# The gV and gK stores of the last head in two parts each: 120 rows and 8 rows

## The chip, the core and the metric

The kernel runs on one core of a Trainium2 chip. The metric is the device time of one execution, in microseconds (us). Engines are named as the profile names them: PE (TensorE matmul) and PEld (its weight loads), DVE (VectorE), ACT (ScalarE), POOL (GpSimd) and SP (SyncE, which here only issues transfers). Sixteen DMA engines move the data between HBM and the core's SBUF (the on-chip memory of 128 partitions). A DMA instruction of any of the issuing engines is cut up over them, and it adds 16 to a semaphore when all of it has landed.

## The reference

The program is the gradient of one decoder block for a single new token: LayerNorm, attention over a cache of 4096 positions, a residual, LayerNorm, a two-layer ReLU network, a residual. There are 2 batch entries, 32 heads of width 128, a model width of 640 and a hidden width of 1728, all in bf16.

```python
scores = jnp.einsum("bhqd,bhkd->bhqk", q, k) * (Dh ** -0.5)
p = _softmax(scores, axis=-1)
o = jnp.einsum("bhqk,bhkd->bhqd", p, v)
...
h  = x + A(_layernorm(x), k_cache, v_cache, wq, wo)
h2 = h + B(_layernorm(h), w1, w2)
...
_out, _vjp = jax.vjp(_f, A_x, A_k_cache, A_v_cache, A_wq, A_wo, B_w1, B_w2)
_grads = _vjp(grad_out)
```

The outputs are `h2` and seven gradients. The two large ones are the gradients of the K cache (`out_2`) and of the V cache (`out_3`), each of 2 x 32 heads x 4096 x 128 bf16. With one query per head they are outer products: for one head, gV is `p` (4096 numbers) times a row of 128 numbers, and gK is the gradient of the scores times the query row.

## The kernel before, in words

A head's 4096 x 128 matrix is 1 MB. It is held as one tile of 128 partitions by 32 x 128 numbers, so that a partition holds 32 consecutive positions, 8192 bytes that are contiguous in HBM (`natural`, line 451).

Pass 1 (`p1_iter`) goes over the 64 heads (`NP1`), reads K and V, forms the scores, the softmax numerators and some sums. A middle part (`middle_gen`) does the network and its gradients. Pass 2 (`p2_iter`, with its delayed second half `p2_tail`) goes over the 64 heads again in the order `turns`; most V tiles are loaded once more ("W"), some were kept. For each head `j` pass 2

- transposes V on PE and multiplies it by the output gradient (`pair_transpose`, `pair_matvec`),
- builds gV on DVE in two halves (`outer_half`, line 832). In the last three heads DVE leaves the last four of the 32 position blocks to ACT (line 899). GpSimd then issues the store of gV to `out_3` (line 900),
- in `p2_tail`, one head later, forms the score gradient `gsp` on DVE (line 843), builds gK in two halves (line 832), and GpSimd issues the store of gK to `out_2` (line 851).

In this way 128 stores of 1 MB go out from GpSimd's queue, gV and gK in turn. The tiles are taken from a set of homes (`take`, `give`) and a home is written again when the store that read it has landed. The framework that records the program gives GpSimd's stores eight semaphores in turn, and has a store wait until the store that used its semaphore before, eight stores earlier, has landed. The last two stores are those of head 63: gV of line 900 at `j == NP1 - 1`, and gK of line 851, which is issued when `p2_tail(NP1 - 1)` runs after the last `p2_iter`.

Beside the two passes, background generators hand out small pieces of work: `fin_gen` makes the weight gradients, stored from ACT's queue, and `gx_gen` makes the gradient of the input and ends with two stores of 5 rows from SP's queue (`store_row`, line 653). When all is issued, SP waits for all outstanding transfers and the engines meet at a barrier (the instructions under line 1288, the kernel's call).

Of the kernel before, what the change touches and what calls it, by code (L numbers as in the profile page):

```python
# [15 lines left out]
def kernel(  # L16
# [20 lines left out]
    nc = tc.nc  # L37
# [36 lines left out]
    def pst(shape, dtype, role, name):  # L74

        k = banks[role].pop(0)
        banks[role].append(k)
        return ps.tile(shape, dtype, tag=f"bank{k}", bufs=1, name=name)
# [11 lines left out]
    def take(tag, shape, name):  # L90
        assert free[tag] > 0, (tag, name)
        free[tag] -= 1
        k = homes[tag].pop(0)
        t = pools[k].tile(shape, BF16, tag=f"big{k}", bufs=1, name=name)
        home_of[id(t)] = (tag, k, t)
        return t
# [9 lines left out]
    def give(t, to=None):  # L106
        tag, k, _ = home_of.pop(id(t))
        to = to or goes_to(tag)
        owned[tag] -= 1
        owned[to] += 1  # L110
        free[to] += 1
        homes[to].append(k)
        given_at[k] = step[0]
# [288 lines left out]
    NP1 = len(pairs)  # L402
# [24 lines left out]
    def pair_transpose(nat, g, dve=False, busy=0):  # L427


        t_ps = pst([128, GT // 2, 128], FP32, "tps", "t_ps")  # L430
        warm(t_ps[:].rearrange("p j k -> p (j k)"), nat, g, busy)
        natf = nat[:].bitcast(FP32)
        for j in range(GT // 2):
            cc = (g * GT) // 2 + j
            nc.tensor.transpose(t_ps[:, j, :], natf[:, 2 * cc:2 * cc + 2, :].rearrange("p c k -> p (c k)"), ident_f[:])  # L435
        t_sb = mats.tile([128, GT // 2, 128], FP32, tag="XT", bufs=4, name="t_sb")
        if dve:
            nc.vector.tensor_copy(out=t_sb[:], in_=t_ps[:])  # L438
        else:
            nc.scalar.copy(out=t_sb[:], in_=t_ps[:])  # L440
        return t_sb

    def pair_matvec(dst, t_sb, g, vecs):
        v = t_sb[:].bitcast(BF16).rearrange("p j (k two) -> p j k two", two=2)
        for j in range(GT // 2):
            sc = g * GT + 2 * j
            for par in range(2):
                nc.tensor.matmul(dst[:, sc:sc + 2], lhsT=v[:, j, :, par], rhs=vecs[:, par, :],  # L448
                                 start=(par == 0), stop=(par == 1))

    def natural(cache, b, h):
        return cache[b, h].rearrange("(p sc) d -> p sc d", sc=NSC)
# [377 lines left out]
    def outer_half(dst, row, colp, k, n=HALF):  # L830
        sl = slice(k * HALF, k * HALF + n)
        nc.vector.tensor_tensor(  # L832
            out=pairs_view(dst[:, sl, :]),
            in0=row.rearrange("p (a two) -> p a two", two=2)[:, None, :, :].to_broadcast([128, n, 64, 2]),
            in1=colp[:, sl, None, :].to_broadcast([128, n, 64, 2]), op=ALU.mult)

    def p2_tail(j):

        p = S2[j]
        bp, hp = turns[j]  # L840
        pair_matvec(p["dp"], p.pop("T3"), 3, gom[:, bp, hp, :, :])
        gsp = small.tile([128, NSC, 2], BF16, tag="gsp", bufs=2, name="gsp")
        nc.vector.scalar_tensor_tensor(
            out=gsp[:], in0=p["dp"][:, :, None].to_broadcast([128, NSC, 2]), scalar=negdot[:, hp, bp:bp + 1],
            in1=P_bf[:, p_slot[(bp, hp)], :, None].to_broadcast([128, NSC, 2]), op0=ALU.add, op1=ALU.mult)
        yield
        gK = take("g", [128, NSC, 128], "gK")
        outer_half(gK, p["rb"][:, 128:256], gsp, 0)
        yield
        outer_half(gK, p["rb"][:, 128:256], gsp, 1)  # L850
        nc.gpsimd.dma_start(out=natural(out_2, bp, hp), in_=gK[:])  # L851
        give(gK)
        del S2[j]
        yield
# [3 lines left out]
    def p2_iter(j, nsb):  # L858

        tail = p2_tail(j - 1) if j - 1 in S2 and "T3" in S2[j - 1] else iter(())  # L860
        c = S2[j]
        next(tail, None)
        b, h = turns[j]
        go = gom[:, b, h, :, :]
        bank = pst([128, 512], FP32, "sps", "dp_ps")
        for k, col in enumerate((goc, qsc)):
            nc.tensor.matmul(bank[:, 128 + k * 128:256 + k * 128],  # L867
                             lhsT=col[:, h, b:b + 1].to_broadcast([128, 128]), rhs=ident_bf[:],
                             start=True, stop=True)
        c["dp"] = bank[:, 0:NSC]  # L870
        rb = mats.tile([128, 256], BF16, tag="rb", bufs=3, name="rb")
        nc.scalar.activation(out=rb[:], in_=bank[:, 128:384], func=ACT.Copy, scale=rt[:, b, h:h + 1])  # L872
        pp = small.tile([128, NSC, 2], BF16, tag="pp", bufs=2, name="pp")
        nc.gpsimd.tensor_copy(out=pp[:], in_=P_bf[:, p_slot[(b, h)], :, None].to_broadcast([128, NSC, 2]))
        if nsb:
            pf = small.tile([128, NSB], FP32, tag="pf", bufs=2, name="pf")
            nc.gpsimd.tensor_copy(out=pf[:, 0:nsb], in_=P_bf[:, p_slot[(b, h)], NSC - nsb:NSC])
        c.update(rb=rb, pp=pp)
        c["T0"] = pair_transpose(c["W"], 0)
        next(tail, None)  # L880
        yield
        for _ in tail:
            yield
        c["T1"] = pair_transpose(c["W"], 1)
        pair_matvec(c["dp"], c.pop("T0"), 0, go)
        yield
        c["T2"] = pair_transpose(c["W"], 2)
        pair_matvec(c["dp"], c.pop("T1"), 1, go)
        yield
        c["T3"] = pair_transpose(c["W"], 3)  # L890
        give(c["W"], "g" if j < H and j != 1 and owned["g"] < 3 else None)
        pair_matvec(c["dp"], c.pop("T2"), 2, go)
        gV = take("g", [128, NSC, 128], "gV")
        outer_half(gV, c["rb"][:, 0:128], c["pp"], 0)
        yield
        outer_half(gV, c["rb"][:, 0:128], c["pp"], 1, HALF - nsb)
        if nsb:
            for k in range(nsb):
                nc.scalar.activation(out=gV[:, NSC - nsb + k, :], in_=rb[:, 0:128], func=ACT.Copy, scale=pf[:, k:k + 1])
        nc.gpsimd.dma_start(out=natural(out_3, b, h), in_=gV[:])  # L900
        give(gV)
        yield

# [266 lines left out]
    for n, (i, j) in enumerate(plan):  # L1170
# [22 lines left out]
        if j is not None:  # L1193
            if j < NP1:
                bg_until(("go", *turns[j]))
            nsb = 0 if i is not None else NSB if j < H and fin is None else NSB // 2 if j >= NP1 - 3 else 0
            g2 = p2_iter(j, nsb) if j < NP1 else p2_tail(NP1 - 1)
        elif open_tail:
            g2 = p2_tail(open_tail[0])
# [93 lines left out]
```

## Time and profile before

| what | us |
|---|---|
| three timed runs: median (lowest to highest) | 898.54 (893.46 to 898.84) |
| the profiled execution, its own time | 896.3 |
| its span, first to last instruction | 894.4 |
| DVE busy | 688.1 (77% of the span) |
| PE busy | 740.6 (83%) |
| ACT busy | 469.5 (52%) |
| POOL busy | 198.6 (22%) |

The page counts 361.84 MB moved in 56304 packets, 405 GB/s on average. In its row of 40 slices the DMA engines show 9 tenths or more in every slice but two, one of 7 in the second quarter and the last one of 6. Reading starts at the DMA side for this reason. The page's times are of one execution. A view by windows gives, for a stretch of time, the busy time of each engine, the granted PE clock and the mean busy share of the 16 DMA engines (a share of 0.0625 is one engine of sixteen).

### The profile page before, as it was taken

How to read it: one execution, taken by the hardware profiler on the slowest of the kernel's cores; microseconds unless marked ns; L12 is line 12 of the kernel's file. 1: busy time of each engine (PE TensorE's matmuls, PEld its weight loads, DVE VectorE, ACT ScalarE, POOL GpSimd, SP SyncE). 2: the span in 40 equal slices, each digit the busy share in tenths (PEclk: the TensorE clock that was granted, in tenths of full speed). 3: DMA queues.
4: the chain of work that ended last, by engine and by line, in shares of the span. 5: the costliest groups of instructions: out<-in, count | busy, mean ns of one | idle time of the engine just before them, and what ended most of it. 6: DMA issues, size and time to landing. Idle time of an engine off the chain costs nothing.

```text
span 894.4 us, 24636 instructions
## 1 busy us (share of the span) xinstructions
PE 740.6 (83%) x10145; PEld 622.7 (70%) x10145; DVE 688.1 (77%) x1283; ACT 469.5 (52%) x1184; POOL 198.6 (22%) x342
## 2 busy tenths in 40 slices
PE   4999899999998998897867887875698988858881
PEld 4887788888887887777757776764566765635570
DVE  2666778976888897796678897877988468898992
ACT  1344334443555665464545776553476666537751
POOL 1344434442210000000011231111222111111141
PEclk9999989999999999898995555555657566555655
DMA  9999999999979999999999999999999999999996
GB/s 377 420 412 403 409 407 418 411 414 410 356 299 366 422 422 424 422 422 423 414 382 390 416 416 418 414 412 422 398 394 423 426 421 424 423 426 424 423 423 256
DMA packets 56304, 361.84 MB, mean 405 GB/s; under 512 B 5696, under 2 KB 11904, under 8 KB 15488
## 3 DMA queue, kind: packets, MB, share of 16 engines
q1 hardware_dynamic: 34536, 211.13, 58.1%
q0 software_dynamic: 18432, 134.23, 36.1%
q10 hardware_dynamic: 3224, 14.92, 4.0%
q8 instruction: 80, 1.31, 0.6%
q14 instruction: 32, 0.26, 0.1%
HBM read 211.11 MB, written 149.13 MB: 403 GB/s over the span
## 4 chain that ended last, share of the span: by engine, by line
DMA 37%; PE 31%; DVE 19%; issue 6%; ACT 3%; POOL 1%; SPq 0%; POOLq 0%; DVEq 0%; ACTq 0%
DMA out_dram<-gK 16%; PE t_ps L435 13%; DMA Vt<-in_A_v_cache_dram 12%; PE m_ps L469 7%; DMA out_dram<-gV 5%; DVE gV L832 5%; DVE gK L832 4%; DVE rows L658 4%; PE s_ps L448 3%; DVE pk L476 3%; DMA wo_t<-in_A_wo_dram 2%; PE u_ps L498 2%; DMA Kt<-in_A_k_cache_dram 2%; PE dp_ps L448 2%; ACT t_sb L440 1%
## 5 line engine op out<-in xcount | busy, mean ns | idle before, releaser
L440 ACT COPY t_sb<-t_ps 128x512 f32<-128x512 f32 x479 | 272.6, 587 | 181.3 <-PE t_ps L435 177.0
L448 PEld LDWEIGHTS <-t_sb 128*128 128x128 bf16 x4096 | 169.7, 103 | 75.1 <-ACT t_sb L440 33.3
L435 PE MATMUL t_ps<-ident_f,Wt 128*128 128x128 f32 x832 | 200.0, 392 | 0.4 <-ACT t_sb L440 0.4
L476 DVE TENSOR_TENSOR pk<-Kt,ep 128x2048 bf16<-128x2048 bf16 x128 | 156.3, 1222 | 44.7 <-ACT ep L523 26.0
L469 PE MATMUL m_ps<-pk,Vt 128*128 128x129 bf16 x2048 | 175.8, 224 | 15.0 <-DMA Vt<-in_A_v_cache_dram 14.4
L832 DVE TENSOR_TENSOR gK<-rb,gsp 128x2048 bf16<-128x2048 bf16 x128 | 153.4, 1224 | 18.5 <-DMA out_dram<-gV 16.9
L832 DVE TENSOR_TENSOR gV<-rb,pp 128x2048 bf16<-128x2048 bf16 (+2 forms) x128 | 147.1, 1172 | 23.6 <-DMA out_dram<-gK 23.1
L435 PEld LDWEIGHTS t_ps<-ident_f,Wt 128*128 128x128 f32 x832 | 140.2, 204 | 32.1 <-issue 26.5
L435 PE MATMUL t_ps<-ident_f,Kt 128*128 128x128 f32 x1024 | 153.4, 285 | 3.7 <-DMA Kt<-in_A_k_cache_dram 3.5
L469 PEld LDWEIGHTS <-Vt 128*128 128x128 bf16 x2048 | 130.9, 100 | 18.1 <-DMA Vt<-in_A_v_cache_dram 16.1
L435 PEld LDWEIGHTS t_ps<-ident_f,Kt 128*128 128x128 f32 x1024 | 116.3, 148 | 5.1 <-issue 2.6
L486 POOL COPY pk<-ep 128x16 bf16<-128x16 bf16 x80 | 83.6, 1047 | 152.3 <-ACT ep L523 107.0
L448 PE MATMUL dp_ps<-gom,t_sb 128*128 128x2 bf16 x2048 | 96.0, 168 | 14.5 <-ACT t_sb L440 14.1
L900 POOL DMA_DIRECT2D out_dram<-gV x64 | 34.3, 536 | 317.7 <-DVE gV L832 115.6
L448 PE MATMUL s_ps<-gom,t_sb 128*128 128x2 bf16 x2048 | 80.2, 164 | 1.2 <-DVE t_sb L438 1.2
L851 POOL DMA_DIRECT2D out_dram<-gK x64 | 34.1, 533 | 200.3 <-DVE gK L832 149.6
L582 ACT CAST MT<-m_ps 128x128 bf16<-128x128 f32 x64 | 17.0, 266 | 116.3 <-PE m_ps L469 116.3
L965 ACT CAST ot<-o_ps 128x512 bf16<-128x512 f32 (+3 forms) x152 | 66.8, 494 | 8.9 <-DMA out_dram<-ot 7.3
L872 ACT ACTIVATE rb<-dp_ps,rt 128x256 bf16<-128x256 f32 x64 | 30.3, 474 | 45.5 <-PE dp_ps L867 43.2
L658 DVE CUSTOM_DVE_ANT_0 rows<-wo_t,rows 128x640 bf16<-128x640 bf16 x64 | 52.3, 818 | 0.2
L658 DVE CUSTOM_DVE_ANT_0 rows<-wqs,gqr 128x1024 bf16<-128x1024 bf16 x40 | 48.8, 1220 | 0.2
L658 DVE CUSTOM_DVE_ANT_0 rows<-w_t,rows 128x640 bf16<-128x640 bf16 (+2 forms) x58 | 45.9, 792 | 2.8 <-ACT rows L636 2.1
(194 smaller groups left out, 715.7 us busy)
## 6 DMA issues: line engine op xcount, KB each, us to landing
Kt<-in_A_k_cache_dram SPq DMA_DIRECT2D x64, 1024.0 KB, 16.5
Vt<-in_A_v_cache_dram SPq DMA_DIRECT2D x64, 1024.0 KB, 16.6
out_dram<-gV POOLq DMA_DIRECT2D x64, 1024.0 KB, 14.1
out_dram<-gK POOLq DMA_DIRECT2D x64, 1024.0 KB, 14.3
Wt<-in_A_v_cache_dram SPq DMA_DIRECT2D x52, 1024.0 KB, 11.4
out_dram<-ot ACTq DMA_DIRECT2D x6, 960.0 KB, 12.7
wq_t<-in_A_wq_dram SPq DMA_DIRECT2D x5, 1024.0 KB, 11.0
wqs<-in_A_wq_dram SPq DMA_DIRECT2D x5, 1024.0 KB, 22.2
```

Source lines behind the costliest of these rows:

```text
L435: nc.tensor.transpose(t_ps[:, j, :], natf[:, 2 * cc:2 * cc + 2, :].rearrange("p c k -> p (c k)"), ident_f[:])
L440: nc.scalar.copy(out=t_sb[:], in_=t_ps[:])
L448: nc.tensor.matmul(dst[:, sc:sc + 2], lhsT=v[:, j, :, par], rhs=vecs[:, par, :], start=(par == 0), stop=(par == 1))
L469: nc.tensor.matmul(r["m"][:, 0:129], lhsT=r["V"][:, sc, :], rhs=r["pk"][sc // HALF][:, sc % HALF, 0:129], start=(sc == 0), stop=(sc == NSC ...
L476: nc.vector.tensor_tensor(out=p["pk"][k][:, :, 0:128].rearrange("p s (a two) -> p s a two", two=2), in0=p["K"][:, sl, :].rearrange("p s (a ...
L486: nc.gpsimd.tensor_copy(out=col, in_=e)
L658: nc.vector.tensor_tensor_reduce(out=junk[0:kc, 0:width], in0=in0, in1=in1, scale=1.0, scalar=0.0, op0=ALU.mult, op1=ALU.add, accum_out=acc)
L832: nc.vector.tensor_tensor(out=pairs_view(dst[:, sl, :]), in0=row.rearrange("p (a two) -> p a two", two=2)[:, None, :, :].to_broadcast([128 ...
L851: nc.gpsimd.dma_start(out=natural(out_2, bp, hp), in_=gK[:])
L872: nc.scalar.activation(out=rb[:], in_=bank[:, 128:384], func=ACT.Copy, scale=rt[:, b, h:h + 1])
L900: nc.gpsimd.dma_start(out=natural(out_3, b, h), in_=gV[:])
L965: nc.scalar.copy(out=ot[0:P, k, n0:n0 + nn], in_=o_ps[0:P, 0:nn])
```

## The change

A helper `store` is added in front of `p2_tail`. For all heads but the last it issues the same single store as before. For the last head it issues two: rows (partitions) 0 to 119, then rows 120 to 127, both from GpSimd's queue.

```diff
+    def store(dst, t, last):
+
+        if not last:
+            nc.gpsimd.dma_start(out=dst, in_=t[:])
+            return
+        for rows in (slice(0, 120), slice(120, 128)):
+            nc.gpsimd.dma_start(out=dst[rows], in_=t[rows])
+
     def p2_tail(j):
...
-        nc.gpsimd.dma_start(out=natural(out_2, bp, hp), in_=gK[:])
+        store(natural(out_2, bp, hp), gK, j == NP1 - 1)
...
-        nc.gpsimd.dma_start(out=natural(out_3, b, h), in_=gV[:])
+        store(natural(out_3, b, h), gV, j == NP1 - 1)
```

In the built program the instructions of PE, DVE and ACT are the same in number, order and waits. GpSimd's last two stores of 128 rows become four, of 120, 8, 120 and 8 rows. They take the next four of the eight semaphores, so that the third one waits for the landing of the gV store of head 60 and the fourth for the gK store of head 60. SP's last wait asks for these two semaphores at the higher count.

## The prediction, written before the changed kernel was run

> **What bounds the kernel at its end.** I began with the critical chain, the work that ended last, because the change touches only the last two of 128 stores. Its end (start us, length us, what):
>
> ```profile
> 873.32 0.91 DVE gV L832
> 874.23 1.80 issue
> 876.03 0.02 POOLq L851
> 876.05 0.53 POOL out_dram L900
> 876.58 1.72 issue
> 878.30 0.56 POOLq L1288
> ```
>
> No engine works after 878.9 but the span ends at 894.4. The last 15.5 us are transfers. The view of waits from 860 to 895 us, for SP's queue, names them (total us, times, longest):
>
> ```profile
> SPq L1288 <- DMA out_dram<-gV: 19.2, 1, 19.2
> SPq L1288 <- DMA out_dram<-gK: 2.4, 1, 2.4
> ```
>
> SP's closing wait ends first on the gV stores, then 2.4 us later on the last gK. The issues of gK (line 851) in this stretch give the times:
>
> ```profile
> L851 POOL DMA_DIRECT2D out_dram<-gK x4: 533/533/533, 864.1 to 878.3; - x4
> ...
> DMA to landing us min/median/max: 14.0/14.1/14.4
> ```
>
> The last gK is issued at 878.3 and lands 14.4 us later, at 892.7; closing takes 1.7 us more, and 1.9 us lie outside the span (896.3 in all). Next, how many of the 16 DMA engines still work. The windows view (stretch, its length, busy time of PE, PEld, DVE, ACT, POOL, granted clock, DMA share, GB/s):
>
> ```profile
> 880.00:882.00 2.00, 0.00 (x0) 0.00 (x0) 0.00 (x0) 0.00 (x0) 0.00 (x0) 0.50 1.00 418
> 882.00:884.00 2.00, 0.00 (x0) 0.00 (x0) 0.00 (x0) 0.00 (x0) 0.00 (x0) 0.50 0.96 406
> 884.00:886.00 2.00, 0.00 (x0) 0.00 (x0) 0.00 (x0) 0.00 (x0) 0.00 (x0) 0.50 0.54 229
> 886.00:888.00 2.00, 0.00 (x0) 0.00 (x0) 0.00 (x0) 0.00 (x0) 0.00 (x0) 0.50 0.17 70
> 888.00:890.00 2.00, 0.00 (x0) 0.00 (x0) 0.00 (x0) 0.00 (x0) 0.00 (x0) 0.50 0.08 33
> 890.00:892.00 2.00, 0.00 (x0) 0.00 (x0) 0.00 (x0) 0.00 (x0) 0.00 (x0) 0.50 0.07 29
> ```
>
> All 16 engines work until 883, half of them are done by 886, and for the last 4 us the share is 0.07, one engine of sixteen. One engine is behind the rest, and its rows of the last gV and gK alone set the end. Followed packet by packet (each starts when its engine's one before ends), the last engine ends at 892.30, the next ones at 888.35, 887.79 and 886.27, the first at 883.29. So the tail is an imbalance of queues, and the question is how many rows the change leaves on that one engine.
>
> **The price of a row.** The page's account of GpSimd's queue:
>
> ```profile
> q0 software_dynamic: 18432, 134.23, 36.1%
> ```
>
> 18432 packets by 128 stores are 144 a store: 128 rows of 8192 bytes and 16 end marks, so 8 rows and a mark for each engine. The 2.4 us between the last two landings are 8 rows on the last engine: 0.31 us a row by its packets (0.309 each, started every 0.306).
>
> **The change, part by part.**
>
> Two more issues on POOL, 0.53 us each. The 8 rows of gV go out at 876.58 to 877.11, inside the 1.72 us in which POOL waits for DVE's second half of gK; the 120 rows of gK still go at 878.33. The 8 rows of gK follow at 878.9 to 879.4, and nothing stands behind them on POOL. Their cover is the backlog: the emptiest DMA engine has rows until 883.3, the last one until it reaches the last gV at 887.4. If these issues took 2 us each, the last would end near 882, still in time. Price 0; without the backlog it would be 0.5.
>
> Two added waits. The third store waits for the gV store of the timeline's first row here, the fourth for the gK store of the second:
>
> ```profile
> 861.45 0.53 POOL L900 DMA_DIRECT2D out_dram<-gV  x1 [2.83 <-DVE gsp L843]
> 861.97 0.73 POOL L874 COPY pp<-P_bf 128x64 bf16<-128x64 bf16 x1
> 862.64 1.18 POOL L877 CAST pf<-P_bf 128x4 f32<-128x4 bf16 x1
> 864.08 0.53 POOL L851 DMA_DIRECT2D out_dram<-gK  x1 [0.25 <-DVE gxo L1059]
> ```
>
> With their 14.1 us to landing these end at 875.6 and at 878.1, before 878.3 and 878.9. The second has only 0.8 us to spare, but only SP's closing wait is behind it, and 4 us of backlog cover a delay. Price 0.
>
> The rows themselves. No row of the trace shows a 120-row or an 8-row store, so I bound it. The count of rows stays 256. If the 120 rows go to 15 engines they are 8 each, as before, and one engine gets none; 8 rows on 8 engines are one more each. The last engine then has 0 to 18 rows of the two stores, where it had 16. The upper end is 2 x 0.306 = +0.6 us. At the lower end its queue ends 16 rows or 4.9 us earlier, 887.4, and the next engine, 888.35 with up to two rows more, 889.0, is last: 892.3 - 889.0 = -3.3 us.
>
> Which end? The nearest rows are the only partial stores near the end, two of 5 rows from SP. In the stretch from 860 to 895 us the account of their queue is
>
> ```profile
> q1 hardware_dynamic: 20, 0.00, 0.0%
> ```
>
> that is 10 packets for each: 5 rows and 5 marks on five engines. Both times they are the same five by the packets, and the last engine is one of them. If GpSimd's partial stores fill engines in the same fixed order, an engine that a 5-row store takes is also among the 15 of a 120-row store and the 8 of an 8-row store. The one left out lies at the other end. So I take the upper end, +0.6 us.
>
> The Trainium skill (DMA: Bandwidth & Descriptors, section Why a DMA increments its semaphore by 16 and not by 1) says that a transfer from SP takes the lowest-numbered engines, as many as divide its rows, and that some GpSimd copies on trn2 put a sixteenth of the partitions, rounded up, on each engine in order, so that 100 partitions leave engine 15 without data. By these two rules 120 rows leave out engine 15, the last engine here is one of 0 to 4, and the sum is the same +0.6.
>
> The Trainium skill's Rules for kernel authors (same title) speak against the change: a transfer split by partitions gains nothing, because the parts share the same engines. With the backlog above, the split would cost the added rows and nothing else.
>
> **Sum.** 896.3 + 0 + 0 + 0.6 = 896.9 us. The profiled execution lies 2.2 below the median of the three runs and 2.8 above the lowest, about the middle of all four, so I leave the sum as it is.
>
> **Rivals.**
>
> *The last engine is spared in both stores.* It is the engine that a 120-row store leaves out. For it: 120 = 15 x 8, so some engine is left out, and an engine that is late in every store of the last heads may stand at a special place, such as the end of the row. Against it: it carries the five-row stores. 896.3 - 3.3 = 893.0 us. The Trainium skill (DMA: Bandwidth & Descriptors, Latency and other measured facts) calls engines 7 and 15 usually the slower ones; if the last engine were 15, this rival would hold.
>
> *It is spared in one store only.* The engine left out moves on from store to store and is the last one in one of the two. It has then 8 rows and up to two more instead of 16: 6 x 0.306 = 1.8 us less, 894.5 us. For it: the gV store of 15 engines and the 8-row store behind it need not begin at the same engine. Against it: by chance alone two stores hit one engine of sixteen 1 time in 8.
>
> *The rows pile up on few engines (slower).* If the number of engines must be a power of two, 120 rows go to 8 engines with 15 each, and the last engine, if it is among them, has 30 + 2 rows instead of 16: 16 x 0.306 = +4.9, 901.2 us. On 4 engines it has 60 + 2: 46 x 0.306 = +14.1, 910.4 us. On one engine 240 rows take 73 us. It counts as slower by over 1% (9.0 us) from 30 rows more on the last engine (30 x 0.306 = 9.2), that is from 5 engines or fewer for 120 rows. For it: every GpSimd store of this trace went to 16 engines, so none shows another number. Against it: SP's 5-row stores used five engines, which is no power of two.
>
> That the change doesn't do what it says is excluded by the order of the built program: four stores in place of two, nothing else moved.
>
> More than 6.7 us can't be gained: the shares from 880 on (1.00 + 0.96 + 0.54 + 0.17 + 0.08 + 0.07) x 2 us sum to 5.6 us of all engines, so even a perfect spread ends at 885.6 instead of 892.3.
>
> **How the numbers follow.** Forecast, the last engine keeps its rows (896.9): 0.54. Spared in both (893.0): 0.30. Spared in one (894.5): 0.10. Piling up: 0.06, of which 0.04 over 1%. The three runs lie from 2.8 below to 2.5 above the profiled one, which gives 890.2 to 899.4 over the first three cases; I take 891.5 to 900.0 for 8 in 10, since few of the spared cases fall on the lowest runs and the mildest piling up reaches 901. 1% (9 us) is about what a measurement of this kernel tells from no change. A gain of that size is beyond the bound above: faster 0.02, for scatter alone. Slower 0.05, the 0.04 above and 0.01 for scatter. Same 0.93.
>
> **What would show it.** POOL: four issues near 876.05, 876.6, 878.3 and 878.9; later times mean that an issue or a wait costs more. Windows: with the forecast the share of 0.07 lasts until about 892.6; if the engine is spared it falls to 0 near 889. Piling up shows as a share of some sixteenths that lasts beyond 893. The prediction is wrong if POOL's issues of 120 rows take over 4 us, if the late engine is another one from run to run, or if the backlog of the last heads differs by more than the rows counted here.

## The result, and the profile after

| | before | with the change |
|---|---|---|
| median of 17 runs each, us | 897.71 (893.46 to 899.05) | 900.22 (897.27 to 903.29) |
| ratio of the runs, 95% interval | | 1.0044 (1.0033 to 1.0054) |
| profiled execution, its own time, us | 896.3 | 898.95 |
| its span, us | 894.4 | 897.2 |

The kernel became slower by 0.44%, which is 4.0 us (0.0044 x 897.7). The two medians lie 2.5 us apart; the text goes by the ratio and its interval. The forecast was +0.6 us, inside 1%. 900.22 lies just above the forecast range.

The page's account of GpSimd's queue, with 64 packets more than before:

```profile
q0 software_dynamic: 18496, 134.23, 36.1%
```

Two more stores with 16 end marks each are 32 of these. The bytes are the same, so the other 32 are small packets too: they fit engines that have no row of a partial store and get a 4-byte packet in the place of each missing row (one engine without its 8 rows and 8 engines without their one row are 16, for two pairs 32). This agrees with 15 engines of 8 rows, and 8 engines of one. So does the count in the kernels below that split the two stores into 112 and 16 or 64 and 64 rows, where every engine can have the same number of rows: 18464, the 32 end marks and nothing more.

The issues of the changed kernel (line 843) and their landing, then the same by size (KB each, median us from issue to landing), from the view of transfers between 860 and 898 us:

```profile
L843 POOL DMA_DIRECT2D out_dram<-gV x2: 511/524/536, 875.0 to 875.5; - x2
L843 POOL DMA_DIRECT2D out_dram<-gK x2: 502/522/543, 877.3 to 877.9; - x2
```

```profile
out_dram<-gV POOLq DMA_DIRECT2D x1, 960.0 KB, 17.3
out_dram<-gK POOLq DMA_DIRECT2D x1, 960.0 KB, 17.7
out_dram<-gV POOLq DMA_DIRECT2D x1, 64.0 KB, 17.1
out_dram<-gK POOLq DMA_DIRECT2D x1, 64.0 KB, 17.5
```

The second issue of a pair goes out 0.52 us after the first, as priced. gV's parts land at 875.0 + 17.3 = 892.3 and 875.5 + 17.1 = 892.6, gK's at 895.0 and 895.4: each 8-row part lands 0.3 us behind its 120 rows. That is one row on the last engine. But the first parts take 17.3 and 17.7 us to land, where the last whole stores of gK before took 14.0 to 14.4. The windows view shows when it goes wrong, first one line of before, then the change:

```profile
878.00:880.00 2.00, 0.00 (x0) 0.00 (x0) 0.03 (x1) 0.00 (x0) 0.53 (x1) 0.50 1.04 434
```

```profile
876.00:878.00 2.00, 0.00 (x0) 0.00 (x0) 1.03 (x1) 0.00 (x0) 0.71 (x3) 0.50 1.05 406
878.00:880.00 2.00, 0.00 (x0) 0.00 (x0) 0.00 (x0) 0.00 (x0) 0.36 (x1) 0.50 0.91 242
880.00:882.00 2.00, 0.00 (x0) 0.00 (x0) 0.00 (x0) 0.00 (x0) 0.00 (x0) 0.50 0.93 254
882.00:884.00 2.00, 0.00 (x0) 0.00 (x0) 0.00 (x0) 0.00 (x0) 0.00 (x0) 0.50 0.88 307
...
888.00:890.00 2.00, 0.00 (x0) 0.00 (x0) 0.00 (x0) 0.00 (x0) 0.00 (x0) 0.50 0.09 33
890.00:892.00 2.00, 0.00 (x0) 0.00 (x0) 0.00 (x0) 0.00 (x0) 0.00 (x0) 0.50 0.06 25
892.00:894.00 2.00, 0.00 (x0) 0.00 (x0) 0.00 (x0) 0.00 (x0) 0.00 (x0) 0.50 0.06 25
894.00:896.00 2.00, 0.00 (x0) 0.00 (x0) 0.00 (x0) 0.00 (x0) 0.00 (x0) 0.50 0.03 12
```

Before, the engines moved 434 and 418 GB/s from 878 to 882. Now they are busy 0.91 and 0.93 of the time and move 242 and 254 GB/s. A busy share that stays while the rate falls means longer packets. By the trace's single packets a row of 8192 bytes took 310 to 316 ns on average in each microsecond from 875 to 883 before, and 526, 453, 472 and 486 ns in the four from 878 on with the change, some of them over 1400 ns.

The landing times of the last stores, from the trace's semaphore records (us, and the step from the store before):

```
             before            with the change
gV head 61   880.51            879.10
gK head 61   882.96  2.45      882.85  3.75
gV head 62   885.41  2.45      886.85  4.00
gK head 62   887.86  2.45      889.64  2.79
gV head 63   890.29  2.43      892.29  2.65, then 8 rows 892.60  0.31
gK head 63   892.72  2.43      895.06  2.46, then 8 rows 895.37  0.31
```

All of these are landings on the last engine. Its whole stores of heads 61 and 62, which the change does not touch, come 1.3, 1.55 and 0.3 us late, while the other engines are at the 120 rows. Over these steps the change is 4.06 us longer: 0.62 for the two extra rows, 3.44 for slowed packets. The two profiled executions differ by only 2.65 us as a whole, because this one reached the tail 1.4 us earlier (879.10 against 880.51), where the change had done nothing yet.

### The profile page after: what moved, and what is told of

The parts are those of the page before. It is cut to its first block, busy times and chain, and to the rows that moved or that the text cites. A ratio compares the mean times of both kernels' runs of the same rounds, so it can differ in the third digit from the quotient of the medians.

```text
span 897.2 us, 24638 instructions
## 1 busy us (share of the span) xinstructions
PE 737.5 (82%) x10145; PEld 617.8 (69%) x10145; DVE 688.7 (77%) x1283; ACT 469.9 (52%) x1184; POOL 197.1 (22%) x344
## 4 chain that ended last, share of the span: by engine, by line
DMA 36%; PE 33%; DVE 18%; issue 6%; ACT 4%; SPq 0%; POOL 0%; DVEq 0%; ACTq 0%; POOLq 0%
DMA out_dram<-gK 16%; PE t_ps L435 14%; DMA Vt<-in_A_v_cache_dram 11%; PE m_ps L469 7%; DMA out_dram<-gV 7%; DVE gK L832 4%; DVE gV L832 4%; DVE rows L658 4%; PE s_ps L448 3%; DVE pk L476 3%; PE u_ps L498 2%; ACT t_sb L440 2%; DMA Kt<-in_A_k_cache_dram 2%; PE dp_ps L448 2%; PE o_ps L967 2%
## 5 line engine op out<-in xcount | busy, mean ns | idle before, releaser
L832 DVE TENSOR_TENSOR gK<-rb,gsp 128x2048 bf16<-128x2048 bf16 x128 | 153.4, 1224 | 22.7 <-DMA out_dram<-gV 20.2
L435 PE MATMUL t_ps<-ident_f,Kt 128*128 128x128 f32 x1024 | 149.8, 281 | 4.9 <-DMA Kt<-in_A_k_cache_dram 4.6
L435 PEld LDWEIGHTS t_ps<-ident_f,Kt 128*128 128x128 f32 x1024 | 113.1, 145 | 6.2 <-issue 3.7
## 6 DMA issues: line engine op xcount, KB each, us to landing
wqs<-in_A_wq_dram SPq DMA_DIRECT2D x5, 1024.0 KB, 20.1
```

The lines of the kernel that those rows point to most:

```text
L832: nc.vector.tensor_tensor(out=pairs_view(dst[:, sl, :]), in0=row.rearrange("p (a two) -> p a two", two=2)[:, None, :, :].to_broadcast([128 ...
```

## The experiments

Each kernel is the changed one with the body of the two-part store replaced, unless the diff says more. Ratios are to the kernel before, on the same chip.

**Issues or layout.** All rows in both parts, split along the positions:

```diff
-        for rows in (slice(0, 120), slice(120, 128)):
-            nc.gpsimd.dma_start(out=dst[rows], in_=t[rows])
+        for part in (slice(0, HALF), slice(HALF, NSC)):
+            nc.gpsimd.dma_start(out=dst[:, part, :], in_=t[:, part, :])
```

> The last gV and gK each go out in two stores of all 128 rows, 16 of the 32 position blocks each (4096 bytes a row and store), so the number of issues, end marks and added waits is that of the change, but every DMA engine keeps the same partitions. Layout theory (a store of 128 rows puts partitions on the DMA engines so that they do not disturb each other, a store of fewer rows does not): as before, ratio 1.000 within 0.15%, DMA share 1.0 with about 420 GB/s until the engines run dry near 883. Issue theory (two more issues, marks and waits cost the 4 us): ratio 1.004 as with the change.

Measured: 1.0003 (0.9989 to 1.0017). Its windows, in place of the 242 and 254 GB/s of the change:

```profile
878.00:880.00 2.00, 0.00 (x0) 0.00 (x0) 0.00 (x0) 0.00 (x0) 0.53 (x1) 0.50 0.98 408
880.00:882.00 2.00, 0.00 (x0) 0.00 (x0) 0.00 (x0) 0.00 (x0) 0.00 (x0) 0.50 0.99 404
```

Two more issues, their marks and the two added waits cost nothing that can be measured, though these parts also have twice as many rows, of half the bytes. Splitting as such is not the cause.

**Extra rows or layout.** Parts in which no engine gets more rows than before:

```diff
-        for rows in (slice(0, 120), slice(120, 128)):
+        for rows in (slice(0, 112), slice(112, 128)):
```

> Parts of 112 and 16 rows: 7 rows and 1 row for each of the 16 engines, so no engine gets more rows than before (16 for the two stores). Rows theory (the late engine pays for its extra rows and nothing else): ratio 1.000. Layout theory: still slower, by about 3 us (1.003 to 1.004), and the rate between 878 and 882 us falls to 250 to 330 GB/s at a DMA share over 0.9, as with the change.

```diff
-        for rows in (slice(0, 120), slice(120, 128)):
+        for rows in (slice(0, 64), slice(64, 128)):
```

> Parts of 64 and 64 rows: 4 rows for each of 16 engines twice, no extra rows. Rows theory: ratio 1.000. Layout theory: each store reads half of the partitions with all 16 engines, which should disturb at least as much as 120 rows: 1.003 to 1.008, rate between 878 and 882 us at or under 300 GB/s. If it is not slower, the disturbance belongs to the uneven counts (120, 112) and not to the layout.

Measured: 1.0044 (1.0032 to 1.0056) for 112 and 16, 1.0035 (1.0021 to 1.0050) for 64 and 64. The windows of the first, then of the second kernel:

```profile
882.00:884.00 2.00, 0.00 (x0) 0.00 (x0) 0.00 (x0) 0.00 (x0) 0.00 (x0) 0.50 1.05 315
884.00:886.00 2.00, 0.00 (x0) 0.00 (x0) 0.00 (x0) 0.00 (x0) 0.00 (x0) 0.50 0.97 303
886.00:888.00 2.00, 0.00 (x0) 0.00 (x0) 0.00 (x0) 0.00 (x0) 0.00 (x0) 0.50 0.89 254
```

```profile
880.00:882.00 2.00, 0.00 (x0) 0.00 (x0) 0.04 (x1) 0.00 (x0) 1.07 (x2) 0.50 1.10 348
882.00:884.00 2.00, 0.00 (x0) 0.00 (x0) 0.00 (x0) 0.00 (x0) 0.00 (x0) 0.50 0.96 258
```

Both are as slow as the change, with the same mark: a share of 0.89 to 1.10 and a rate that falls to 254 and 258 GB/s. These two executions issued their last stores 3 to 4 us later, so the fall comes later. The number of rows on an engine, the only term of the forecast, explains little of the 4 us.

**HBM side or SBUF side.** The last gV and gK as whole stores, but written with twice the distance in HBM, over the places of two earlier heads; this kernel leaves head 63's own places unwritten:

```diff
+    def wide(out):
+        return out[0, H - 6:H - 4].rearrange("h (p two sc) d -> (h p) two sc d", two=2, sc=NSC)[:, 0]
...
-        store(natural(out_2, bp, hp), gK, j == NP1 - 1)
+        store(natural(out_2, bp, hp) if j < NP1 - 1 else wide(out_2), gK, False)
```

and the same for gV and `out_3`.

> The last gV and gK go out whole (128 rows) but to every second 8192-byte row of a region twice as large, over two heads that were stored long before; head 63's own place in both outputs stays unwritten. The engines keep their partitions, and neighbouring engines write HBM 64 KB apart instead of 32 KB, which is the distance of the 120-row store if each engine takes 8 rows in a line. HBM theory (the new distance of the writes slows the packets): ratio 1.003 to 1.004 and a rate under 330 GB/s near 880 us. Layout theory on the SBUF side: as before, ratio 1.000 within 0.15%.

Measured: 1.0002 (0.9986 to 1.0017).

```profile
880.00:882.00 2.00, 0.00 (x0) 0.00 (x0) 0.00 (x0) 0.00 (x0) 0.00 (x0) 0.50 1.01 422
882.00:884.00 2.00, 0.00 (x0) 0.00 (x0) 0.00 (x0) 0.00 (x0) 0.00 (x0) 0.50 1.02 426
```

The distance of the writes in HBM is not it. The next candidate is which partitions the engines read at the same time.

**Which partitions.** Only 64 rows of the last three heads, in two choices of the same size:

```diff
-        for rows in (slice(0, 120), slice(120, 128)):
+        for rows in (slice(32, 96),):
...
-        store(natural(out_2, bp, hp), gK, j == NP1 - 1)
+        store(natural(out_2, bp, hp), gK, j >= NP1 - 3)
```

and the same for gV; the sibling has `slice(0, 64)`.

> For the last three heads only the middle 64 rows (partitions 32 to 95) of gV and gK are stored, in one store each from GpSimd; the other half of these rows is left out. Each of 16 engines has 4 rows of a store, in a line. Pairing theory (partitions p and p + 32 of one half of the SBUF, in groups of four, share one way out; in a whole store one engine reads both groups, and a partial store lets two engines read them at once): rows 32 to 95 hold one group of each of the 16 pairs, so nothing is shared: packets stay near 311 ns, the rate stays near 415 GB/s until the engines run dry, and with 24 rows less on the late engine the run is about 7 us shorter than before (0.991 to 0.994). If any store of 64 rows disturbs, it is like its sibling of rows 0 to 63.

> As its sibling, but rows 0 to 63: the same number of rows, stores, engines and bytes, the same distance of 32 KB between the engines' writes in HBM. Pairing theory: these rows hold both groups of 8 pairs, so 16 engines meet on 8 ways: mean packets over 400 ns, a rate of 200 to 300 GB/s after about 874 us, and a run 3 to 8 us longer than that of rows 32 to 95 (0.995 to 1.002 of before). Theory of partial stores as such: equal to its sibling within 0.2%.

Measured: 0.9922 (0.9902 to 0.9942) for rows 32 to 95, 0.9975 (0.9960 to 0.9990) for rows 0 to 63: 0.0053 x 895.9 = 4.7 us between them, in the predicted direction and size. Windows of rows 32 to 95, then of rows 0 to 63:

```profile
874.00:876.00 2.00, 0.00 (x0) 0.00 (x0) 1.97 (x4) 0.23 (x1) 0.50 (x1) 0.78 0.79 328
876.00:878.00 2.00, 0.00 (x0) 0.00 (x0) 0.93 (x1) 0.00 (x0) 0.50 (x1) 0.50 0.79 328
```

```profile
878.00:880.00 2.00, 0.00 (x0) 0.00 (x0) 1.93 (x2) 0.00 (x0) 0.53 (x1) 0.50 0.81 193
880.00:882.00 2.00, 0.00 (x0) 0.00 (x0) 0.43 (x1) 0.00 (x0) 0.55 (x1) 0.50 0.89 197
882.00:884.00 2.00, 0.00 (x0) 0.00 (x0) 0.00 (x0) 0.00 (x0) 0.00 (x0) 0.50 0.89 209
```

Rows 32 to 95 move 328 / 0.79 = 415 GB/s per unit of share, the full rate; their engines only lack work. Rows 0 to 63 move 209 / 0.89 = 235, little over half. By single packets a row takes 309 to 318 ns on average in each microsecond from 870 to 884 with rows 32 to 95, and 443 to 618 ns from 871 to 886 with rows 0 to 63. Bytes, issues and HBM distances are equal, and the HBM addresses differ only by a shift of 256 KB, so the difference lies in the SBUF partitions. It also shows that a partial store is not slow as such. The Trainium skill (SBUF — State Buffer, Door 1: The DMA port swizzle) gives the map: partitions p and p + 32 in groups of four share one of 16 ports, 0 to 63 reach 8 ports and, by its table, 32 to 95 all 16; it quotes 196 GB/s for 64 partitions from 0 at 1 MiB. The trace agrees with 193 to 209 GB/s from 878 to 884. For the parts of 120 and 112 rows the cause is inferred: if the engines of a partial store take rows in a line, 7 or 8 each, two of them meet at one port. The records here do not name the engine of a packet, so no run shows this order directly.

**Who issues.** The last two stores from SP's queue, whole (one `dma_start` of all rows) and in the two parts, whose diff is:

```diff
-            nc.gpsimd.dma_start(out=dst[rows], in_=t[rows])
+            nc.sync.dma_start(out=dst[rows], in_=t[rows])
```

> The last gV and gK go out whole but from SP's queue in place of GpSimd's. They take turns with GpSimd's backlog on each engine, whose rows are as many as before: 1.000 within 0.2%. It is the control for the next run.

> The parts of 120 and 8 rows as in the change, from SP's queue. Layout theory (it matters which engine reads which partitions, not who issues): slower than the whole stores from SP by about 3 to 4 us, 1.003 to 1.0045 of before, the rate between 878 and 884 us under 330 GB/s. If GpSimd's way of making descriptors is what disturbs: 1.000 within 0.2%.

Measured: 1.0004 (0.9992 to 1.0016) whole, 1.0014 (1.0002 to 1.0027) in parts. This was half a miss. The rate does fall with the parts from SP too, where the whole stores from SP moved 430 and 369 GB/s:

```profile
880.00:882.00 2.00, 0.00 (x0) 0.00 (x0) 0.00 (x0) 0.00 (x0) 0.00 (x0) 0.50 0.89 279
882.00:884.00 2.00, 0.00 (x0) 0.00 (x0) 0.00 (x0) 0.00 (x0) 0.00 (x0) 0.50 0.94 299
```

but the end moves by 0.1% only, 0.9 us, which the two intervals do not tell from nothing. The landings tell why the end escapes: from gV of head 61 (880.18) to gK of head 62 (893.00) the last engine's three whole stores take 12.82 us, which is 3 x 2.45 and 18 rows of 0.304 from SP between them. In the whole version four stores and 16 such rows take 14.66 = 4 x 2.45 + 4.86. So here the last engine paid for its two extra rows (0.6 us) and lost nothing to slow packets; others did, and one of them ends at 893.32, 0.3 us after it. From SP the partial rows take turns with GpSimd's backlog on each engine and do not follow it. That this order spares the last engine is a reading that was not tried. The page counts 34838 packets in SP's queue, against 34824 with the whole stores: 14 more, which fits 15 and 8 end marks for each of the two pairs in place of 16.

**Half of it.** Only gK, and only gV, in two parts (`False` in place of `j == NP1 - 1` for the other):

> Only the last gK goes out in 120 and 8 rows; the last gV is whole. Layout theory: half of the change: one row more on the late engine (0.3 us) and the slowing of one store in place of two (about 1.7 us), 1.001 to 1.003. If the gV parts alone do it, because the engines still have their whole stores to send beside them: under 1.001. If one split is enough to spoil the rest: 1.004.

> Only the last gV goes out in 120 and 8 rows; the last gK is whole. The split of gK alone cost 0.1%, a quarter of the change. If the parts of gV do most of it, since their rows go out while all engines still have whole stores to send: 1.0025 to 1.004. If each split alone is cheap and only the two together are dear: 1.000 to 1.0015.

Measured: gK alone 1.0011 (0.9995 to 1.0027), gV alone 1.0015 (1.0002 to 1.0028). In the traces the end comes 20.2 and 20.1 us after the issue of gK of head 62, against 19.0 before and 22.6 with both. So each costs 1.1 to 1.2 us and the two together more than the sum, by one trace of each kernel. The intervals of the timed ratios do not show that last point: 0.0026 with an error of about 0.002 stands against 0.0044 with 0.001. Neither guess of the second expectation was met clearly.

**All of it.** Every store of pass 2 in 120 and 8 rows:

```diff
-        if not last:
-            nc.gpsimd.dma_start(out=dst, in_=t[:])
-            return
```

> All 128 stores of pass 2 go out in 120 and 8 rows. Layout theory: each store slows the packets beside it as the last two did, and since the DMA engines are busy all through pass 2 nothing hides it: between q0's 36% of the DMA time taking 1.35 times as long (1.12) and 2 us for each of 128 stores (1.28); at least 1.08. If the slowing only counts at the end of the kernel, where nothing follows: 1.004 to 1.02.

Measured: 1.0985 (1.0941 to 1.1029), 87 us between the medians or 0.7 us for each of 128 stores. The windows view from 600 to 700 us, before and in this kernel:

```profile
600.00:700.00 100.00, 75.94 (x738) 59.19 (x738) 82.76 (x143) 56.43 (x127) 22.30 (x39) 0.60 1.01 411
```

```profile
600.00:700.00 100.00, 65.79 (x593) 51.87 (x594) 75.97 (x128) 44.76 (x96) 27.30 (x55) 0.53 0.94 345
```

The DMA engines are taken almost all the time in both, and move 345 in place of 411 GB/s. All compute engines but POOL do less. Per unit of share it is 367 in place of 407 GB/s, so longer packets are the larger part; the share itself falls from 1.01 to 0.94, and why was not separated: twice as many stores also share the eight semaphores. The cost lies above the least that was expected (1.08) and below the range (1.12 to 1.28).

**The late engine.** The last eight heads' stores whole, from SP:

```diff
-        for rows in (slice(0, 120), slice(120, 128)):
-            nc.gpsimd.dma_start(out=dst[rows], in_=t[rows])
+        nc.sync.dma_start(out=dst, in_=t[:])
...
-        store(natural(out_2, bp, hp), gK, j == NP1 - 1)
+        store(natural(out_2, bp, hp), gK, j >= NP1 - 8)
```

> The last eight heads' 16 stores go out whole from SP's queue, which has no loads left by then. If what holds the late engine up is GpSimd's queue (its descriptors or marks), it catches up by some of its 4 us: 0.996 to 0.999. If it is late because of its own share of rows and earlier delays: 1.000 within 0.2%.

Measured: 1.0003 (0.9989 to 1.0017), but not for the reason expected.

```profile
860.00:865.00 5.00, 0.66 (x3) 0.66 (x4) 4.74 (x10) 0.00 (x0) 0.36 (x2) 0.50 0.47 199
...
885.00:890.00 5.00, 0.00 (x0) 0.00 (x0) 2.01 (x2) 0.00 (x0) 0.00 (x0) 0.50 1.01 421
890.00:895.00 5.00, 0.00 (x0) 0.00 (x0) 0.00 (x0) 0.00 (x0) 0.00 (x0) 0.50 0.28 118
```

All 16 engines work until 890, and 13 of the 16 end marks of the last store land from 891.59 to 891.75, the last one at 893.32: no engine is 4 us behind any more. But from 860 to 875 the shares are 0.47, 0.88 and 0.85 where they were 1.00, 1.00 and 1.02 before. That is 5 x (0.53 + 0.12 + 0.17) = 4.1 us of all engines, as much as the late engine was behind. Why the stores came late there was not looked into. A version that keeps the even end without the hole might gain the 4 us of the late engine; it was not tried, and no kernel here that stores all rows beat the one before.

## Why the prediction was wrong, point by point

- *What bounds the end.* Right: the last engine's queue sets the end of the changed kernel, 6.0 us behind the next one (895.37 and 889.38). It is less alone in other runs; with only gK in parts the next engine is 0.6 us behind (893.84 and 893.25). One reading was off without touching the sum: "half of them are done by 886" takes the mean share from 884 to 886 for its end. The share of 0.17 from 886 to 888 is under three engines of sixteen.
- *Two issues and two waits at 0.* Right: 0.52 us each, at 875.5 and 877.9, and the split along the positions, with the same issues and waits, gave 1.0003. The backlog covered them as reckoned.
- *Who carries the rows.* Right: 15 engines and 8 engines, the last one among both, with 8 + 1 rows for each store. The two steps of 0.31 us are the +0.6 us of the sum. The two rivals in which it is spared fall.
- *The rows themselves.* This step failed. It said "8 each, as before", counted the rows of an engine and took 0.306 us a row from whole stores, for the partial stores and for the whole ones beside them. It did not ask which partitions an engine gets. In the changed kernel rows took 450 to 530 ns on average from 878 to 882. The runs show that this depends on which partitions are stored; that in the 120 rows two engines meet at one way out of the SBUF is the reading of it. The slowed packets were left out of the sum without a reason, and they measured 3.4 us. "The added rows and nothing else" is the same step.
- *The backlog as cover.* It covered issues, but the backlog is also what is slowed: the last engine's whole stores of heads 61 and 62 came 3.2 us late while it looked safe.
- *The slower rival.* Its sign and nearly its size came true (+4.9 us against +4.0), by coincidence, for its mechanism did not: rows did not pile up on few engines. 64 and 64 rows use all 16 engines and cost the same. The test against it, that SP's 5-row stores use five engines, said nothing of partitions.
- *What would show it.* The share of one engine was to end near 892.6 and lasted to about 895. One of the prediction's signs of being wrong came: the backlog of the last heads differed by more than the rows counted. The sign to look for was the rate beside the share, which no step named.
- *The range.* It came from the scatter of runs and the row counts, and its upper end of 900.0 lacked the slowed packets. The sum also started from one execution of 896.3, 1.4 us under the median of 17 runs, so of the 3.3 us between 896.9 and 900.22 that much is the starting point.

## What to carry to other kernels

Count which SBUF partitions are read at the same time, not only how many rows each DMA engine has: a store of fewer than 128 partitions can run at half the rate and slow the whole stores beside it, and 64 rows from 32 on moved at the full rate where 64 rows from 0 moved at little over half. If a store has to be split, split it along the free dimension (1.0003 here), not by partitions (1.0035 to 1.0044, and 1.0985 when every store was split). When a DMA share stays near 1 and GB/s falls, look at the length of single packets, and at which partitions are read at the same time.

## What the runs showed of the hardware that was not expected

- A partial store slows transfers that have nothing to do with it: rows of 8192 bytes beside it went from 311 to about 500 ns, single ones to 1479 ns.
- Engines that have no row of a partial GpSimd store seem to get a 4-byte packet for each row they lack: 64 packets more for two stores split into 120 and 8 rows, 32 more for 112 and 16 or 64 and 64, and 22528 in place of 18432 when all 128 were split, 48 for each in place of 16 beside the rows.
- One DMA engine was 3.7 to 4.2 us behind the next one at the end of the kernel before and of those with 4096-byte halves, with the wide distance and with 64 and 64 rows, 6.0 us with the change, but only 0.6 to 1.4 us with 112 and 16 rows or with one split store. It was 0.3 us when the last 16 stores came from SP. Where it falls behind was not looked into.
